# The end of a linear-attention and spectral-mixing kernel: eight tiles finished singly, the last mode's products with repeated columns, no 8 KB stores

## Chip, cores, metric

One core of one Trainium2 chip. The metric is the device time of one execution in microseconds (us), the median of several. A profile is one execution recorded instruction by instruction; its span (first to last instruction) is 1.7 to 1.8 us shorter than the device time. The granted clock is the share of its full clock that TensorE was given at a moment, as the profile records it (1.00 or 0.50 here). PE is TensorE, DVE is VectorE, ACT is ScalarE, POOL is GpSimd, SP issues the stores.

## The reference, cut to what matters

```python
# q, k, v: [8 batches, 8 heads, 576, 64];  w_r, w_i: [64 modes, 512, 512];  w_ch: [512, 512]
q_p, k_p = phi(q), phi(k)                       # elu + 1
num = q_p @ (k_p^T v);  den = q_p . sum(k_p) + 1e-6
x = (num / den)                                 # [8, 576, 512]
X = rfft(x, axis=1)[:, :64]                     # 64 modes
Y = X * (w_r + i w_i)                           # one 512x512 complex product for each mode
u = x + irfft(Y, n=576)
out = u + maximum(u @ w_ch, 0)                  # float32
```

The mode weights are 134 MB in float32. Loading them fills most of the time: their last packet lands at 387.69 us of 419.6. What is left after the last weights have landed is a chain: the last mode's product, its way through the inverse transform, the sums of all output tiles, and 9.4 MB of stores.

Of the kernel before, what the change touches and what calls it, by code (L numbers as in the profile page):

```python
# [10 lines left out]
F32 = mybir.dt.float32  # L11
# [32 lines left out]
def kernel(  # L44
# [10 lines left out]
    nc = tc.nc  # L55

    B, H, S, Dh = q.shape
    D = H * Dh
    NM = moe_w_r.shape[0]
    NHP = H // 2  # L60
    NDC = D // 128
    NJJ = 4
    NDW = 4 * NDC
    NDL = NDW // 2
    NMP = NM // 2
    XDC = 2 * B * NMP
    NL = 8
# [24 lines left out]
    def xt_cols(dc: int, kk: int, n: int):  # L92

        dc = (dc // NDC * 2 + kk % 2) * NDC + dc % NDC
        c0 = dc * XDC + kk // 2
        return xt_c[:, c0 : c0 + (n - 1) * NMP + 1 : NMP]
# [6 lines left out]

    W_KEEP = 2
    pin = tc.keep_in_program_order
    PIECES = (slice(0, 4), slice(4, 6), slice(6, 7), slice(7, 8))
    HALVES = [slice(0, 64), slice(64, 128)]

    LAST = NM // 2 - 1
# [11 lines left out]
    def w_load_last(pool, tag: str, bufs: int):  # L121
        w_in[LAST] = pool.tile([128, NDW, D], BF16, tag=tag, bufs=bufs, name=f"w{LAST}")
        for g in range(2):
            for half in range(2):
                rows_in = (moe_w_r, moe_w_i)[half][NM - 2 + g].rearrange("(p dc) e -> p dc e", dc=NDL)
                for dcs in PIECES if (g, half) == (1, 1) else (slice(0, NDL),):
                    dst = w_in[LAST][half::2, g * NDL + dcs.start : g * NDL + dcs.stop]
# [22 lines left out]
    def rows_of(jj: int, base: int = 0):  # L150

        if jj < NJJ:
            return slice(base + jj, base + 512, NJJ)
        return slice(512, S) if base == 0 else slice(0, base)
# [252 lines left out]
    def w_get(p: int):  # L407
        if p not in w_in and p == LAST:
            w_load_last(wpool, "w", W_KEEP)
        elif p not in w_in:  # L410
            for half in range(2):
                w_load(p, half, wpool, "w", W_KEEP)
        return w_in[p]

    def keep_warm(n: int):

        for _ in range(n):
            pin(nc.tensor.matmul(last_ps[0], id16, wch16[:, 0, :]))  # L418
# [4 lines left out]
    def work_slot(p: int, name: str):  # L423
        for _ in range(slots.get((p, name), 0)):
            if work:
                work.pop(0)()

    def product(P, x, n: int, w, dc: int, n_dc: int):
        c = dc % NDC * 32
        pin(  # L430
            nc.tensor.matmul(  # L431
                P[c : c + n, :], x, w[:, dc, :],
                start=(dc < NDC), stop=(dc >= n_dc - NDC), tile_position=(0, c),
                skip_group_check=True,
            )
        )
# [6 lines left out]
    def evacuate(p: int, P):  # L443
        st = ystage.tile([128, D], F16, tag="ystage", bufs=2, name=f"ys{p}")
        if p % 2 == 0:
            pin(nc.vector.tensor_copy(out=st, in_=P))  # L446
        else:
            pin(nc.scalar.copy(out=st, in_=P))  # L448
        return st

    def picks(kk: int, st, n: int):
        for ec in range(NDC):
            pin(
                nc.tensor.matmul(  # L454
                    yt_ps[:, ec, kk % 8 : kk % 8 + n, :].rearrange("p m n -> p (m n)"),
                    st[:, ec * 128 : ec * 128 + 128],
                    pick_sb[:, 0 : n * 2 * B],
                )
            )
# [24 lines left out]
    def last_pair():  # L484
        w = w_get(LAST)
        kk = NM - 2
        work_slot(LAST, "start")
        P = psW.tile([128, D], F32, tag="P", bufs=2, name=f"P{kk}")
        for dc in range(NDL):
            n = 32 if dc < NDC else 2 * B  # L490
            product(P, xt_cols(dc, kk, n), n, w, dc, NDL)
        st = evacuate(kk, P)
        work_slot(LAST, "mid")
        picks(kk, st, 1)
        pin(nc.vector.tensor_copy(out=Y8[:, :, 0 : NL - 1, :], in_=yt_ps[:, :, 0 : NL - 1, :]))
        keep_warm(3)
        kk = NM - 1
        y_last = psW.tile([128, NDC, 2 * B], F32, tag="P", bufs=2, name="y_last")
        for dc in range(NDL):
            for ec in range(NDC):  # L500
                pin(
                    nc.tensor.matmul(
                        y_last[:, ec, :], w[:, NDL + dc, ec * 128 : ec * 128 + 128],
                        xt_cols(dc, kk, 2 * B),
                        start=(dc == 0 and ec == 0), stop=(dc == NDL - 1), skip_group_check=True,
                    )
                )
        nc.vector.tensor_copy(out=Y8[:, :, NL - 1, :], in_=y_last)

    while pending:  # L510
        w_next()
# [7 lines left out]
    psW = tc.alloc_tile_pool(name="psW", bufs=1, space=PSUM, side="left")  # L519
# [13 lines left out]
    Y8 = ystage.tile([128, NDC, NL, 2 * B], F16, name="Y8")  # L533
# [27 lines left out]
    def x_of(t: int):  # L561
        if t < B * NJJ:
            return x_main[t // NJJ][:, t % NJJ, :]
        i = t - B * NJJ
        return x_tail[i // 2][:, i % 2, :]
# [37 lines left out]
    def parts_of(t: int):  # L603
        if t < B * NJJ:
            b, jj = divmod(t, NJJ)
            return [(b, jj, slice(0, 128))]
        p = t - B * NJJ
        return [(2 * p + h, NJJ, HALVES[h]) for h in range(2)]
# [123 lines left out]
    def add_inverse(n: int, half: int, tiles_of=(0, 1)):  # L732

        def mm(i, orow, l, r):
            on_bank(
                n, {i},
                nc.tensor.matmul(  # L737
                    accs[n][orow, i], l, r, start=False, stop=True, skip_group_check=True
                ),
            )  # L740

        for i in tiles_of:
            for b, jj, orow in parts_of(pairs[n][i]):
                sel_rows = rows_of(jj, BASE[b % 2])
                if n < 2 * N_LEAD:
                    mm(i, orow, lead_sb[b][:, sel_rows], last[:, half, :])
                else:
                    g = HALVES[i]
                    mm(i, orow, inv2_sb[g, sel_rows], YZ[b][g, half, :])

    pairs = []
# [9 lines left out]
    def on_bank(n: int, banks: set, ins):  # L761
        pin(ins)
        for other, theirs in users.setdefault(n, []):
            if not banks & theirs:
                tc.declare_no_dep(ins.ins, other.ins, reason="the other bank of the pair")
        users[n].append((ins, banks))
    accs: dict[int, object] = {}

    def channels(n: int):
        pool = acc_pools[n % 4 // 2]  # L770
        accs[n] = pool.tile([128, 2, D], F32, tag="acc", bufs=2, name=f"acc{n}")
        for i, t in enumerate(pairs[n]):
            for cols, src in e0_parts(t):
                on_bank(
                    n, {i},
                    nc.tensor.matmul(  # L776
                        accs[n][:, i, cols], id16, src, start=(cols.start == 0), stop=False,
                        skip_group_check=True,
                    ),
                )  # L780

    def rectified(n: int):
        add_inverse(n, 1)
        for i in range(2):
            a = accs[n][:, i]
            on_bank(n, {i}, nc.scalar.activation(out=a, in_=a, func=AF.Relu))
# [13 lines left out]
            in_=x_tail[i // 2],  # L800
        )

    QUADS = (6, 7)

    def finish(n: int):
        acc = accs[n]
        t0 = pairs[n][0]
        add_inverse(n, 0)
        x = x_main[t0 // NJJ][:, t0 % NJJ : t0 % NJJ + 2, :] if t0 < B * NJJ else x_tail[(t0 - B * NJJ) // 2]
        on_bank(n, {0, 1}, nc.vector.tensor_tensor(out=x, in0=acc, in1=x, op=ALU.add))  # L810
        if t0 < B * NJJ and t0 // NJJ in QUADS:
            if t0 % NJJ:
                store(t0 - 2, NJJ)
            return
        store(t0, 2)
# [106 lines left out]
    for h, eng in enumerate((nc.sync, nc.gpsimd)):  # L922
        eng.dma_start(
            out=YZ_all[64 * h : 64 * h + 64 : NF // NL].rearrange("r b z d -> r b (z d)"),
            in_=last.rearrange("p z d -> p (z d)"),
# [6 lines left out]
    def relu(n: int, i: int):  # L932
        a = accs[n][:, i]
        on_bank(n, {i}, nc.scalar.activation(out=a, in_=a, func=AF.Relu))

    def add_one(n: int, i: int):
        t = pairs[n][i]
        on_bank(n, {i}, nc.vector.tensor_tensor(out=x_of(t), in0=accs[n][:, i], in1=x_of(t), op=ALU.add))
        store(t, 1)

    add_inverse(0, 1, (1, 0))
    on_bank(
        0, {0},
        nc.vector.scalar_tensor_tensor(
            out=x_of(0), in0=accs[0][:, 0], scalar=0.0, in1=x_of(0), op0=ALU.max, op1=ALU.add
# [1 line left out]
    )  # L947
    store(0, 1)
    relu(0, 1)
    rectified(1)  # L950
    add_inverse(0, 0, (1,))
    channels(2)
    add_one(0, 1)
    rectified(2)
    for i in range(2):
        add_inverse(1, 0, (i,))
        add_one(1, i)
    channels(3)
    rectified(3)
    finish(2)  # L960
    for n in range(4, len(pairs)):
        channels(n)
        rectified(n)
        finish(n - 1)
# [32 lines left out]
```

## The kernel before: the parts that the change and the argument touch

The transformed x lies in one tile, with the modes innermost, so the 16 columns that belong to one mode (8 batches, real and imaginary) are 32 elements of two bytes apart:

```python
xt_c = xpool.tile([128, NDW * XDC], BF16, name="xt_c")
xt_v = xt_c.rearrange("p (c t b m) -> p c t b m", c=NDW, t=2, b=B)     # m innermost, NMP = 32 of them

def xt_cols(dc, kk, n):
    dc = (dc // NDC * 2 + kk % 2) * NDC + dc % NDC
    c0 = dc * XDC + kk // 2
    return xt_c[:, c0 : c0 + (n - 1) * NMP + 1 : NMP]                 # step NMP
```

The weights of the last mode come in pieces, and its products use the weights as the stationary operand and 16 columns as the moving one. Before the products stand three fillers (`keep_warm`: products of 128x512 whose result nobody reads):

```python
PIECES = (slice(0, 4), slice(4, 6), slice(6, 7), slice(7, 8))          # of 8 row blocks
...
        keep_warm(3)
        kk = NM - 1
        y_last = psW.tile([128, NDC, 2 * B], F32, tag="P", bufs=2, name="y_last")
        for dc in range(NDL):                                          # 8 row blocks
            for ec in range(NDC):                                      # 4 column blocks
                pin(nc.tensor.matmul(
                        y_last[:, ec, :], w[:, NDL + dc, ec * 128 : ec * 128 + 128],
                        xt_cols(dc, kk, 2 * B),
                        start=(dc == 0 and ec == 0), stop=(dc == NDL - 1), skip_group_check=True))
        nc.vector.tensor_copy(out=Y8[:, :, NL - 1, :], in_=y_last)
```

Then the tiles of the output are finished: tiles 0 to 3 one by one, all later ones in pairs (n numbers the pairs). `channels(n)` puts the product with w_ch into PSUM, `add_inverse(n, 1)` adds the last modes' share to it, `relu` rectifies, `add_inverse(n, 0)` adds the inverse transform, and `add_one` or `finish` adds all that to x and stores it. Pairs 0 and 1 (tiles 0 to 3) take the last mode from `last`, with 128 rows; later ones take it from `YZ`, with 64 rows: one product of a pair reads rows 0 to 63, the other rows 64 to 127, and in the trace the two start 4 ns apart (394.706 and 394.710 us, L737).

```python
    QUADS = (6, 7)                     # batches whose four tiles are stored in one 1 MB transfer
    ...
    store(0, 1)
    relu(0, 1)
    rectified(1)                       # add_inverse(1, 1) and relu for both tiles of the pair
    add_inverse(0, 0, (1,))
    channels(2)
    add_one(0, 1)
    rectified(2)
    for i in range(2):
        add_inverse(1, 0, (i,))
        add_one(1, i)
    channels(3)
    rectified(3)
    finish(2)
    for n in range(4, len(pairs)):
        channels(n)
        rectified(n)
        finish(n - 1)
    finish(len(pairs) - 1)
```

## Time and profile before

| | before |
|---|---|
| device time, first three runs | 421.33, 421.40, 422.91 us |
| span of the profiled execution | 419.6 us |
| last packet of the weights | 387.69 us |
| copy of the last mode's product starts | 388.32 us |
| first store of output issued | 391.68 us |
| VectorE's last sum ends | 413.73 us |
| last store packet ends | 418.22 us |

The rows are moments of one execution, counted from its first instruction. Read them as a chain: what the loads leave, the single file through the engines (388 to 391.7), and the stores. The prediction below shows the lines that these moments come from. Two lines more are needed for later, from the order of TensorE's instructions: four small products (`yt`, 16 columns of two bytes that lie side by side) and the 32 products of the last mode, 16 columns each. In the single instructions the first follow each other at 25 ns and the second at 28.

```profile
385.97 0.26 PE L454 MATMUL yt<-pick_sb,ys 128*128 128x16 f16 x4
386.79 1.50 PE L502 MATMUL y_last<-xt_c,w 128*128 128x16 bf16 x32
```

### The profile page before, as it was taken

What the parts mean: (1) busy time and instruction counts of PE and PEld (TensorE: products, weight loads), DVE (VectorE), ACT (ScalarE), POOL (GpSimd) and SP (SyncE); (2) the same over time, 40 slices, a digit from 0 to 9 for tenths busy, and PEclk for the clock granted to TensorE, in tenths of its full rate; (3) what the DMA queues carried; (4) which work ended last, traced back from release to release, by engine and by line L of the source; (5) the groups of instructions that cost most, each with busy time, mean ns of one, the idle gap of its engine ahead of it and who ended that gap; (6) DMA issues with size and microseconds to landing.
All of it is one profiled execution on the core that took longest, in us unless ns stands there. A gap on an engine that the chain in (4) does not pass through costs nothing.

```text
span 419.6 us, 7393 instructions
## 1 busy us (share of the span) xinstructions
PE 289.5 (69%) x3118; PEld 157.0 (37%) x3118; DVE 227.9 (54%) x495; ACT 154.1 (37%) x253; POOL 57.5 (14%) x99
## 2 busy tenths in 40 slices
PE   0359799999607553444343686998798877899992
PEld 0248677787301221222121232433343324364420
DVE  3588979994404462464645353454455433612794
ACT  4677788954101011000000233344253422230782
POOL 4122224210001111111111111111111111130000
PEclk9999958989555555555555589799899989999997
DMA  8999999999999999999999999999999999998698
GB/s 217 211 212 217 209 223 204 227 206 225 216 221 212 215 220 211 219 217 211 223 214 212 223 214 211 223 215 212 221 214 214 219 214 217 219 208 162 229 402 322
DMA packets 16417, 93.17 MB, mean 222 GB/s; under 512 B 2032, under 2 KB 2944, under 8 KB 11968
## 3 DMA queue, kind: packets, MB, share of 16 engines
q0 software_dynamic: 12416, 81.48, 93.3%
q1 hardware_dynamic: 3968, 11.22, 7.1%
q8 instruction: 24, 0.39, 0.3%
q14 instruction: 9, 0.07, 0.0%
HBM read 163.93 MB, written 9.44 MB: 413 GB/s over the span
## 4 chain that ended last, share of the span: by engine, by line
DMA 68%; PE 19%; DVE 4%; issue 3%; POOL 3%; ACT 2%; DVEq 0%; ACTq 0%; POOLq 0%
DMA w<-in_moe_w_i_dram 53%; DMA pick_sb<-row_pick 8%; PE P L431 7%; DMA k<-in_k_dram 7%; PE acc L737 3%; PE acc L776 2%; POOL w L116 2%; PE kvp L256 1%; ACT ke L207 1%; DVE x L292 1%; PE zl L418 1%; PE yt L454 1%; PE xp L322 0%; ACT ys L448 0%; PE num L162 0%
## 5 line engine op out<-in xcount | busy, mean ns | idle before, releaser
L431 PE MATMUL P<-w,xz 128*32 128x512 bf16 x496 | 48.3, 529 | 63.9 <-DMA w<-in_moe_w_i_dram 61.5
L448 ACT CAST ys<-P 128x512 f16<-128x512 f32 x15 | 8.8, 586 | 131.4 <-PE P L431 131.4
L116 POOL DMA_DIRECT2D w<-in_moe_w_r_dram x31 | 17.8, 576 | 244.1 <-PE P L431 240.6
L431 PEld LDWEIGHTS <-xz 128*32 128x32 bf16 x496 | 13.2, 115 | 85.0 <-DMA w<-in_moe_w_i_dram 56.4
L446 DVE CAST ys<-P 128x512 f16<-128x512 f32 x17 | 11.8, 691 | 54.1 <-PE P L431 54.1
L678 PE MATMUL eps<-wch,xTw 128*128 128x512 f16 x144 | 40.6, 409 | 0.0
L162 PEld LDWEIGHTS <-qT 64*128 64x128 f16 (+1 forms) x640 | 22.8, 124 | 31.7 <-issue 17.3
L661 ACT CAST x16w<-x_main 128x512 f16<-128x512 f32 x32 | 19.8, 618 | 37.6 <-DVE x_main L659 37.6
L659 DVE TENSOR_TENSOR x_main<-ya,x_main 128x512 f32<-128x512 f32 x32 | 22.0, 691 | 18.8 <-PE ya L655 18.6
L256 PE MATMUL kvp<-vpad,ke 32*128 32x130 f16 x576 | 23.4, 256 | 8.9 <-ACT qT L243 6.1
L441 DVE COPY xz<-xt_c 64x256 bf16<-64x256 bf16 x62 | 23.0, 370 | 11.5 <-PE P L431 10.7
L686 ACT CAST E<-eps 128x512 f16<-128x512 f32 (+1 forms) x40 | 21.2, 540 | 19.5 <-PE eps L678 19.5
L256 PEld LDWEIGHTS <-ke 32*128 32x128 f16 x576 | 21.5, 113 | 10.6 <-issue 8.5
L162 PE MATMUL nw<-kv,qT 64*128 64x65 f16 (+1 forms) x320 | 18.9, 240 | 9.5 <-DVE x_tail L622 4.5
L418 PE MATMUL zl<-wch,id 128*128 128x512 f16 x96 | 23.1, 380 | 0.0
L292 DVE TENSOR_TENSOR x<-num,rd 128x512 f16<-128x512 f32 x32 | 22.1, 692 | 1.1
L236 PE MATMUL qTp<-id,qe 128*128 128x128 f16 x144 | 14.2, 277 | 12.0 <-DVE qe L220 9.7
L207 ACT ACTIVATE qe<-q 128x1152 f16<-128x1152 f16 (+1 forms) x16 | 17.9, 1157 | 7.6 <-DMA q<-in_q_dram 7.5
L622 DVE TENSOR_TENSOR x_main<-nw,rd 128x256 f32<-128x256 f32 x32 | 11.2, 415 | 17.4 <-PE nw L162 17.4
L670 DVE COPY xTw<-xTp 128x512 f16<-128x512 f16 x36 | 15.0, 416 | 10.0 <-PE xTp L668 9.9
L454 PE MATMUL yt<-pick_sb,ys 128*128 128x32 f16 (+1 forms) x128 | 8.8, 186 | 16.2 <-DMA pick_sb<-row_pick 10.1
L243 ACT COPY qT<-qTp 128x1152 f16<-128x1152 f16 x16 | 19.6, 1289 | 0.4 <-PE qTp L236 0.2
(117 smaller groups left out, 492.9 us busy)
## 6 DMA issues: line engine op xcount, KB each, us to landing
w<-in_moe_w_r_dram POOLq DMA_DIRECT2D x31, 1024.0 KB, 12.5
w<-in_moe_w_i_dram POOLq DMA_DIRECT2D x31, 1024.0 KB, 16.8
out_dram<-x_main SPq DMA_DIRECT2D x10, 512.0 KB, 4.0
k<-in_k_dram POOLq DMA_DIRECT2D x8, 576.0 KB, 12.8
v<-in_v_dram POOLq DMA_DIRECT2D x8, 576.0 KB, 14.2
q<-in_q_dram POOLq DMA_DIRECT2D x7, 576.0 KB, 12.5
out_dram<-x_main SPq DMA_DIRECT2D x2, 1024.0 KB, 4.6
q<-in_q_dram SPq DMA_DIRECT2D x2, 576.0 KB, 4.7
```

Of the source, the lines that this page charges most:

```text
L116: nc.gpsimd.dma_start(out=w_in[p][half::2], in_=two.rearrange("g (r dc) e -> (g r) dc e", dc=NDW))
L162: mm = nc.tensor.matmul(num[hpo][orow, c0 : c0 + 65], qT[rows, hpp, h2, cols], kv_sb[rows, hpp, h2, :])
L207: pin(nc.scalar.activation(out=ev[:, c], in_=heads(nm, b, c), func=AF.Exp))
L256: nc.tensor.matmul(kv_ps[:, h2, 0:130], phi["k", b][r0 : r0 + 32, j // NJ, j % NJ].rearrange("p o d -> p (o d)"), vp[r0 : r0 + 32, :, j, 0 ...
L292: nc.vector.tensor_tensor(out=dst.rearrange("p (o c d) -> p o c d", o=2, c=4), in0=nv[:, :, :, 0:64], in1=rden.unsqueeze(3).broadcast_to([ ...
L418: pin(nc.tensor.matmul(last_ps[0], id16, wch16[:, 0, :]))
L431: nc.tensor.matmul(P[c : c + n, :], x, w[:, dc, :], start=(dc < NDC), stop=(dc >= n_dc - NDC), tile_position=(0, c), skip_group_check=True,)
L441: pin(nc.vector.tensor_copy(out=xz[p % 2][HALVES[h], :, h, :], in_=src))
L659: pin(nc.vector.tensor_tensor(out=x, in0=acc, in1=x, op=ALU.add))
L661: pin(nc.scalar.copy(out=x16w[t], in_=x))
L678: nc.tensor.matmul(e_ps, xT[:, c, :], wch16[:, c, :], start=(c == 0), stop=(c == NDC - 1))
L686: pin(nc.scalar.copy(out=dst, in_=e_ps[:, cols]))
```

## The change

Its parts: (1) tiles 0 to 7 are finished singly, with the sums made ahead by a few tiles, and pairs come after; (2) the last mode's products take their 16 columns six times over (96 columns, of which only the first 16 results are used), and a filler is put behind them; (3) the last piece list starts with two smaller pieces; (4) no batch waits for all four of its tiles to be stored in runs of 8 KB. What each part aims at is not written in the kernel; the names suggest that the repeats and the filler are to keep TensorE's clock up, and the singles to bring the stores forward.

```diff
-    PIECES = (slice(0, 4), slice(4, 6), slice(6, 7), slice(7, 8))
+    PIECES = (slice(0, 2), slice(2, 4), slice(4, 6), slice(6, 7), slice(7, 8))
@@
-        y_last = psW.tile([128, NDC, 2 * B], F32, tag="P", bufs=2, name="y_last")
+        n_rep = 6
+        y_last = psW.tile([128, NDC, n_rep, 2 * B], F32, tag="P", bufs=2, name="y_last")
         for dc in range(NDL):
+            x = xt_cols(dc, kk, 2 * B).unsqueeze(1).broadcast_to([128, n_rep, 2 * B])
             for ec in range(NDC):
                 pin(
                     nc.tensor.matmul(
-                        y_last[:, ec, :], w[:, NDL + dc, ec * 128 : ec * 128 + 128],
-                        xt_cols(dc, kk, 2 * B),
+                        y_last[:, ec], w[:, NDL + dc, ec * 128 : ec * 128 + 128], x,
@@
-        nc.vector.tensor_copy(out=Y8[:, :, NL - 1, :], in_=y_last)
+        keep_warm(1)
+        nc.vector.tensor_copy(out=Y8[:, :, NL - 1, :], in_=y_last[:, :, 0, :])
@@
-    QUADS = (6, 7)
+    QUADS = ()
@@  (channels() may now be called for one tile of a pair)
+    def sums_of(n: int, i: int):
+        channels(n, (i,))
+        add_inverse(n, 1, (i,))
+        relu(n, i)
@@
-    rectified(1)
-    add_inverse(0, 0, (1,))
-    ... (down to finish(2), as above)
+    for i in range(2):
+        add_inverse(1, 1, (i,))
+        relu(1, i)
+    singles = [(0, 1)] + [(n, i) for n in (1, 2, 3) for i in range(2)]
+    ahead = [(n, i) for n in (2, 3, 4) for i in range(2)] + [(5, 0)]
+    for n, i in singles:
+        add_inverse(n, 0, (i,))
+        if ahead:
+            sums_of(*ahead.pop(0))
+        add_one(n, i)
+    finish(4)
+    sums_of(5, 1)
+    for n in range(6, len(pairs)):
```

More of the change, by code (lines that the diff above doesn't have):

```diff
@@ L767, with channels @@
     accs: dict[int, object] = {}
-    def channels(n: int):
-        pool = acc_pools[n % 4 // 2]
-        accs[n] = pool.tile([128, 2, D], F32, tag="acc", bufs=2, name=f"acc{n}")
-        for i, t in enumerate(pairs[n]):
+    def channels(n: int, tiles_of=(0, 1)):
+        if n not in accs:
+            accs[n] = acc_pools[n % 4 // 2].tile([128, 2, D], F32, tag="acc", bufs=2, name=f"acc{n}")
+        for i in tiles_of:
+            t = pairs[n][i]
             for cols, src in e0_parts(t):
@@ L949 @@
     relu(0, 1)
-    rectified(1)
-    add_inverse(0, 0, (1,))
-    channels(2)
-    add_one(0, 1)
-    rectified(2)
-    for i in range(2):
-        add_inverse(1, 0, (i,))
-        add_one(1, i)
-    channels(3)
-    rectified(3)
-    finish(2)
-    for n in range(4, len(pairs)):
+    for i in range(2):
+        add_inverse(1, 1, (i,))
[10 more added lines that the diff above has]
+    for n in range(6, len(pairs)):
         channels(n)
```

## The prediction

> **What bounds the kernel now.** I read the page's slices first (where is the transfer side not full?), then the chain of waits, then stretches of the end, then the order of VectorE's work there.
>
> ```profile
> DMA  8999999999999999999999999999999999998698
> GB/s 217 211 212 217 209 223 204 227 206 225 216 221 212 215 220 211 219 217 211 223 214 212 223 214 211 223 215 212 221 214 214 219 214 217 219 208 162 229 402 322
> DMA 68%; PE 19%; DVE 4%; issue 3%; POOL 3%; ACT 2%; DVEq 0%; ACTq 0%; POOLq 0%
> ```
>
> For 37 of 40 slices (10.5 us each) the transfers are full. These are loads: 164 MB are read from memory at 413 GB/s over the span, and landed narrower. The dips are in slices 37, 38 and 40. The change edits nothing before the last pair of modes, so some 385 of the 421.4 us are out of its reach. In 1 us stretches the loads fall off from 384 on and end at 387.7; the stores run until 418.2. So I cut the end there:
>
> ```profile
> core 0: us, PE busy (x) PEld busy (x) DVE busy (x) ACT busy (x) POOL busy (x), PEclk, DMA share, GB/s
> 384.00:388.00 4.00, 3.96 (x50) 1.74 (x48) 1.32 (x2) 0.00 (x0) 0.00 (x0) 1.00 0.50 92
> 388.00:391.60 3.60, 3.02 (x23) 1.87 (x24) 1.85 (x4) 1.97 (x5) 0.57 (x1) 1.00 0.01 2
> 391.60:396.00 4.40, 4.40 (x21) 1.84 (x19) 3.55 (x6) 3.70 (x8) 0.00 (x0) 1.00 1.02 328
> 396.00:396.50 0.50, 0.50 (x5) 0.15 (x4) 0.50 (x1) 0.24 (x2) 0.00 (x0) 1.00 0.85 303
> 396.50:410.75 14.25, 14.25 (x82) 3.73 (x80) 14.14 (x13) 12.77 (x24) 0.00 (x0) 1.00 1.01 401
> 410.75:414.00 3.25, 1.26 (x8) 0.33 (x6) 2.94 (x3) 1.13 (x3) 0.00 (x0) 1.00 0.96 386
> 414.00:417.50 3.50, 0.00 (x0) 0.00 (x0) 0.00 (x0) 0.00 (x0) 0.00 (x0) 0.60 1.00 404
> ```
>
> The last two columns are to be read. From 388 to 391.6 nothing moves: the last mode's result goes through PE, DVE and ACT one after the other. From 391.6 to the end the transfers are full (1.02, 1.01, 1.00), short only at 396.0 (0.85) and around 411 to 414 (0.96). VectorE is also busy for 14.14 of 14.25 us. Which of the two sets the end? VectorE's last sum ends at 413.7, the transfers go on for 4 us more without a gap, so they do. The sums come in this order (start, duration):
>
> ```profile
> 391.79 0.69 DVE L938 TENSOR_TENSOR x_main<-acc,x_main 128x512 f32<-128x512 f32 x1
> 392.87 1.29 DVE L938 TENSOR_TENSOR x_main<-acc,x_main 128x512 f32<-128x512 f32 x2 [0.39 <-PE acc L737]
> 394.38 6.10 DVE L810 TENSOR_TENSOR x_main<-acc,x_main 128x1024 f32<-128x1024 f32 x5 [0.22 <-PE acc L737]
> ```
>
> One tile costs 0.69, a pair 1.22. A pair is 512 KB, so VectorE offers 524/1.22 = 430 GB/s and the stores take about 401: once behind, the stores stay behind. The hole at 396.0 is where they had caught up: the first whole pair was stored only at 395.63.
>
> And the last mode, in the chain of waits:
>
> ```profile
> 386.89 1.07 PE y_last L502 x28
> 388.00 0.30 PE y_last L502 x4
> 388.32 0.23 DVE Y L508
> ```
>
> In the single instructions, products start 28 ns apart, with breaks at 387.21 to 387.37, 387.59 to 387.67 and 387.77 to 387.99, each before the products of the next piece. The last piece's last packet ended at 387.69. So the last landing (387.99), not PE, sets this step.
>
> [...] the granted clock is 1.00 or 0.50, and it was 1.00 from 343 to 414.7. So in this execution a filler has nothing to win. [...] The trace has 28 ns at 16 columns and 56 ns at 128 [...] here 0.30 us lie between the last packet and its first product (387.69 to 387.99). [...] 84 ns for 2 KB, 160 for 4 KB, 312 for 8 KB (medians of the packet records).
>
> **The change part by part.**
>
> Smaller first pieces. The last 512 KB of weights come in 256, 128, 64, 64 KB; now the first is cut in two. In the packet records of that load, 4 KB packets took 324 ns and 2 KB packets 173, so each pair costs 22 ns more: 64 packets over 16 engines, 4 each, 0.09 us, and one more 22 ns semaphore write: +0.11 us on the last landing. What it gives: products of the first two of eight row blocks can start earlier. But PE works on the filler of three until 386.72, and the whole 256 KB piece had landed by 386.7, so nothing is gained there.
>
> Repeated columns. Six copies of the 16 columns: products 42.5 apart instead of 28.4. The 28 before the last landing still fit between landings (eight take 0.34 us; their room is 0.3). After the last landing: 3 x 14 ns, and 80 columns more to stream in the last product, 33 ns: +0.08 us. The filler, one product of 128x512 (0.22 us), lies in the 0.3 us in which PE waits for VectorE's copy: 0. Sum for the last mode: about +0.17 us (0.11 + 0.08, a little of it overlapped).
>
> Eight tiles singly. Today the singles are tiles 0 to 3, then 7 pairs and more. After: 7 additions of 0.69 (4.83) and 14 pairs of 1.22 (17.1), 21.9 us; before: 3 of 0.69 and 16 pairs, 21.6. So VectorE has 0.3 us more work, but loses its waits of 0.39 and 0.22, because the next tile's sums are now made between one tile's end and the next. PE needs about 3 x 0.215 = 0.65 us for a tile, just under 0.69. Net: VectorE ends within 0.3 us of where it did. For the stores: 256 KB come each 0.69 us, 380 GB/s, and behind the 512 KB rearrangement copies this is enough to keep a queue. The hole at 396 (0.85 of 0.5 us in the window; 12.3 and 9.2 of 16 engines in its two halves, so 0.16 us) and a shortfall at 397.75 (0.03) should go. The price: 4 tiles x 128 packets of 2 KB at 84 instead of half as many at 160: 512 x 4.3 ns / 16 = +0.14 us.
>
> No 8 KB runs. The hold-back of 1 MB ends, so the dips at 410.75 and 413.5 (0.08 + 0.03 us) should go. Price: 256 packets of 8 KB (mean 318) become 512 of 4 KB (164): 512 x 164 - 256 x 318, over 16: +0.16 us by means, +0.1 by medians.
>
> Sum: +0.17 (start of the stores) - 0.30 (holes) + 0.25 (packets) = +0.1 us.
>
> **Rivals.**
> First, that the transfers aren't the limit, but VectorE's stream with its two waits, or the wait for whole pairs. For it: VectorE is as full as the stores, and the chain of waits runs over PE and DVE from 390 to 413. Against it: 4 us of full transfers after its last sum. If true, the end moves by the waits and by the smaller last store (512 KB for 1 MB, 1.3 us): 420 to 420.5.
>
> Second, that timed runs often lose the clock here. For it: one of three runs took 422.91, 1.5 us more; half clock over the PE work from 388 to 394 would cost about that[...]. Against it: nobody profiled that run, and the median was a good one. If true, the median hardly moves and the high runs go: 421.0 to 421.4. The reverse is possible too: a median of three that draws two high ones reads 422.8.
>
> Third, that one late transfer engine sets the end. The stores' last semaphores come at 417.4 to 417.6 from most engines, but at 418.22 from one. The lag appears near 407 and 414, beside 8 KB instruction fetches. A busy engine can't make up for it, so filling holes helps this engine less, and its end would be 0.2 to 0.5 later: 421.7 to 421.9.
>
> **Range and chances.** The sum says 421.5. I lean 0.3 below, to 421.2, because the first two rivals both point down and such parts are seldom kept in a tuned kernel unless they paid. Each term is 0.1 to 0.3 us, the late engine adds 0.4 either way, and a clock lost in two runs adds 1.5: 420.2 to 422.2. A change of 2% is 8.4 us, while the whole edited stretch with empty or dipping transfers is under 6 us: faster by over 2% 0.01, slower 0.01, within 0.98.
>
> **What would show it.** Right: the last mode's copy to Y ends 0.1 to 0.2 later against the last landing; the transfers' share between 392 and 417 has no dip; single sums follow each other without waits; VectorE still ends 3 us or more before the stores. Wrong: the stores begin earlier than 3.9 us after the loads' last packet; VectorE's last sum is over 0.5 us earlier and the end follows it; the granted clock falls to 0.50 before the last stores; or the loads themselves end over 0.5 us elsewhere than at 387.7, which none of my steps foresees.

## The result, and the profile after

The changed kernel took 426.81 us (median of 6 runs, 426.27 to 430.75), the kernel before 421.41 us (6 runs, 421.33 to 423.26). The ratio is 1.0138, with a 95% interval of 1.0093 to 1.0184. Ratios here are the mean time of one kernel's fast runs over that of the other's of the same rounds, so not quite the ratio of the medians quoted. By the 2% rule that is "same", but 5.4 us slower is far outside the range on record.

| moment, us | before | after | difference |
|---|---|---|---|
| last packet of the weights | 387.69 | 387.64 | -0.05 |
| copy of the last mode's product starts | 388.32 | 392.02 | +3.70 |
| first store of output issued | 391.68 | 396.85 | +5.17 |
| VectorE's last sum ends | 413.73 | 420.08 | +6.35 |
| last store packet ends | 418.22 | 423.87 | +5.65 |
| span | 419.6 | 425.3 | +5.7 |

So the loads are unchanged and nothing is lost before them. Of 5.65 us, 3.70 are lost between the landing of the weights and the copy, another 1.47 on the way from the copy to the first store, and 0.48 among the stores. The chain of waits of the changed kernel names the first (start, us, what):

```profile
386.76 5.22 PE y_last L504 x32
391.98 0.43 PE zl L418
392.41 0.50 PE ypl L911 x4
392.91 0.85 PE zl L917 x4
393.76 0.85 PE z1l L917 x4
```

The 32 products took 5.22 us in one unbroken piece, where the prediction allowed them 42.5 ns each, 1.4 us. In the single instructions they start 163 or 164 ns apart (the first gap alone is 145), without a break for any piece of weights. The transposes behind them (`ypl`) took 0.50 and the two groups of four products 0.85 each, for 0.40, 0.44 and 0.45 before. The clock differs; two stretches of the changed kernel, the products and the way to the first store (the third column from the right is the granted clock):

```profile
core 0: us, PE busy (x) PEld busy (x) DVE busy (x) ACT busy (x) POOL busy (x), PEclk, DMA share, GB/s
386.60:391.80 5.20, 5.20 (x33) 3.71 (x32) 0.16 (x1) 0.00 (x0) 0.00 (x0) 0.86 0.08 13
391.98:396.35 4.37, 4.34 (x19) 2.22 (x18) 1.43 (x4) 1.70 (x4) 0.57 (x1) 0.50 0.00 0
```

PE reads as fully busy in both, and yet the clock was cut to 0.50 at 390.34, still within the slow products, and given back at 397.16. A busy share of 5.20 of 5.20 us did not keep the clock here. Note also that the products' spacing did not change at 390.34: at half the clock they were still 163 ns apart, while the products of 256 dense columns behind them (`zl`) started 213 ns apart at 0.50, for 109 at 1.00 in the kernel before. So the granted clock was not what paced the slow products.

In VectorE's order in the changed kernel (some lines between are left out), the first line is the copy, the rest are the tiles' sums:

```profile
392.02 0.22 DVE L510 CAST Y<-y_last 128x64 f16<-128x64 f32 x1 [5.26 <-PE y_last L504]
396.13 0.69 DVE L952 SCALAR_TENSOR_TENSOR x_main<-acc,x_main 128x512 f32<-128x512 f32 x1 [0.35 <-PE acc L739]
397.37 3.28 DVE L941 TENSOR_TENSOR x_main<-acc,x_main 128x512 f32<-128x512 f32 x5 [0.55 <-PE acc L739]
400.85 0.69 DVE L941 TENSOR_TENSOR x_main<-acc,x_main 128x512 f32<-128x512 f32 x1 [0.20 <-PE acc L739]
401.75 0.69 DVE L941 TENSOR_TENSOR x_main<-acc,x_main 128x512 f32<-128x512 f32 x1 [0.20 <-PE acc L739]
404.29 2.51 DVE L813 TENSOR_TENSOR x_main<-acc,x_main 128x1024 f32<-128x1024 f32 x2 [0.52 <-PE acc L739]
```

The bracket is VectorE's idle time before the line and what ended it. Five single sums do run back to back (3.28 us for five), as the change wants, but waits of 0.20, 0.20 and 0.52 us come after them, all for TensorE. This raises a second suspicion: is the new order of the end a cost of its own?

### The profile page after: what moved, and what is told of

Its sections match the earlier page's. It is cut to its first block, busy times and chain, and to the rows that moved or that the text cites.

```text
span 425.3 us, 7406 instructions
## 1 busy us (share of the span) xinstructions
PE 302.1 (71%) x3119; PEld 164.7 (39%) x3119; DVE 228.7 (54%) x497; ACT 154.7 (36%) x253; POOL 58.5 (14%) x100
## 4 chain that ended last, share of the span: by engine, by line
DMA 66%; PE 22%; DVE 3%; issue 2%; POOL 2%; ACT 2%; DVEq 0%; ACTq 0%; POOLq 0%
DMA w<-in_moe_w_i_dram 51%; DMA pick_sb<-row_pick 8%; PE P L431 7%; DMA k<-in_k_dram 7%; PE acc L739 3%; PE kvp L256 2%; PE acc L779 2%; POOL w L116 2%; PE y_last L504 1%; ACT ke L207 1%; PE qTp L236 1%; PE zl L418 1%; DVE x L292 1%; PE xf L354 1%; PE yt L454 0%
## 5 line engine op out<-in xcount | busy, mean ns | idle before, releaser
L256 PE MATMUL kvp<-vpad,ke 32*128 32x130 f16 x576 | 25.3, 273 | 8.8 <-ACT qT L243 5.9
L256 PEld LDWEIGHTS <-ke 32*128 32x128 f16 x576 | 23.4, 122 | 10.5 <-issue 8.6
L236 PE MATMUL qTp<-id,qe 128*128 128x128 f16 x144 | 16.0, 300 | 11.5 <-DVE qe L220 9.6
L162 PE MATMUL num<-kv,qT 64*128 64x65 f16 (+1 forms) x320 | 16.4, 222 | 5.2 <-DVE x L292 3.0
```

Source lines behind the costliest of these rows:

```text
L162: mm = nc.tensor.matmul(num[hpo][orow, c0 : c0 + 65], qT[rows, hpp, h2, cols], kv_sb[rows, hpp, h2, :])
L236: nc.tensor.transpose(qT_ps[:, j], phi["q", b][:, c, j].rearrange("p o d -> p (o d)"), id16,)
L256: nc.tensor.matmul(kv_ps[:, h2, 0:130], phi["k", b][r0 : r0 + 32, j // NJ, j % NJ].rearrange("p o d -> p (o d)"), vp[r0 : r0 + 32, :, j, 0 ...
```

## The experiments

Theories. A: the repeated columns cost nearly all of it. A1: because the moving operand's columns lie 64 bytes apart, each takes four times as long as a dense one; A2: because of the number of columns or the zero step of the repeat (the same addresses are read again). B: the new order of the end costs a good part. C: the half clock is a consequence of the slow products and costs about 2 us on top. The last mode's part and the rest of the change are separated first.

### 16 columns again, all else as changed (rep1)

```diff
-        n_rep = 6
+        n_rep = 1
```

> The changed kernel with the columns of the last mode's products not repeated (16 columns again, as before), all else as changed. Theory A (the 32 products with repeated columns cost the time: they took 5.2 us for 1.4, 163 ns each where I had estimated 42.5, and the half clock that followed came of it): 421.0 to 421.9 us, products 28 ns apart, clock 1.00 until the stores. Theory B (the new order of the end, singles for pairs, costs a good part, since VectorE waited after 400.6): 423.5 us or more.

Measured: 421.71 us (6 runs, 421.63 to 423.79) against 421.6, ratio 0.9995 [0.9964, 1.0026]. The products were 28 ns apart again, the copy started at 388.33, the first output store was issued at 391.69 and the clock stayed at 1.00 to 417. Theory A holds: without the repeats the loss is gone, and what the other parts do together is below what these runs resolve.

The run also isolates the order of the end, with the clock full. VectorE's order in this run:

```profile
391.80 3.28 DVE L941 TENSOR_TENSOR x_main<-acc,x_main 128x512 f32<-128x512 f32 x5
395.28 0.69 DVE L941 TENSOR_TENSOR x_main<-acc,x_main 128x512 f32<-128x512 f32 x1 [0.20 <-PE acc L739]
396.17 0.69 DVE L941 TENSOR_TENSOR x_main<-acc,x_main 128x512 f32<-128x512 f32 x1 [0.20 <-PE acc L739]
398.72 2.51 DVE L813 TENSOR_TENSOR x_main<-acc,x_main 128x1024 f32<-128x1024 f32 x2 [0.52 <-PE acc L739]
```

The waits of 0.39 and 0.22 at the first tiles are gone as predicted, but the same three new waits as above stand at later tiles. TensorE's order shows the reason:

```profile
394.19 0.38 PE L779 MATMUL acc<-E,id 128*128 128x512 f16 x1
394.50 0.40 PE L739 MATMUL acc<-YZ_all,inv_sb 64*128 64x512 f16 x1
394.84 0.41 PE L739 MATMUL acc<-last,lead_sb 128*128 128x512 f16 x1
395.08 0.38 PE L779 MATMUL acc<-E,id 128*128 128x512 f16 x1
```

From one `acc<-E` to the next, one tile's three products, pass 0.89 us (394.19 to 395.08); VectorE needs 0.69 for a tile. The product of 64 rows is what stretches it: 0.31 from the product before it and 0.34 to the next, where full products follow each other at 0.216. The kernel before has a pair at this place, whose two 64-row products start 4 ns apart:

```profile
394.71 0.41 PE L737 MATMUL acc<-YZ_all,inv_sb 64*128 64x512 f16 x2
395.05 0.62 PE L737 MATMUL acc<-last,lead_sb 128*128 128x512 f16 x2
```

The pair has the same 0.31 before it (the last `acc<-E` starts at 394.40) and the same 0.34 behind it. So the added time lies at the changes between 128 and 64 rows; a pair meets them once for two tiles, singles once for each. VectorE's last sum ended at 414.51, 0.78 later than before. The stores hid nearly all of it: their last packet ended at 418.37 against 418.22.

### The repeats alone on the kernel before (only_reps)

The edit is part (2) of the change alone, the repeats and the filler.

> The kernel before with the repeated columns and the filler behind them, nothing else of the change. Theory A: 426 to 427.5 us, nearly the whole loss, products 163 ns apart. Theory B: under 424.5 us, the rest being due to the order of the end.

Measured: 427.11 us (6 runs, 426.05 to 429.46), ratio 1.0125 [1.0091, 1.0159]. The products were 162 to 165 ns apart after a first gap of 145, and the clock fell to 0.50 at 392.77, again within the slow products. (The profiled execution, 429.46 us, is of a slower group of times that is explained below; its products began at 389.25.) Part (2) alone gives the whole loss; the other direction of the same statement as the run before, and theory B falls as an explanation of it.

### The same 96 columns from a dense tile (dense6)

```diff
+    xd = ystage.tile([128, NDL, 2 * B], BF16, name="xd")
+    for dc in range(NDL):
+        pin(nc.vector.tensor_copy(out=xd[:, dc, :], in_=xt_cols(dc, NM - 1, 2 * B)))    # long before
@@
-            x = xt_cols(dc, kk, 2 * B).unsqueeze(1).broadcast_to([128, n_rep, 2 * B])
+            x = xd[:, dc, :].unsqueeze(1).broadcast_to([128, n_rep, 2 * B])
```

> The changed kernel, but the 16 columns of each row block are first gathered into a dense tile (eight small VectorE copies long before), and the products repeat those six times: the same 96 columns, the same zero step of the repeat. Theory A1 (it is the 64-byte step between columns [...]): products 42 to 44 ns apart, 421.0 to 422.0 us, clock 1.00 through. Theory A2 (it is the number of columns, or the repeat itself): products still near 163 ns, 426 to 427.5 us.

Measured: 423.93 us median, but in two groups: 421.75 and 421.86, and four runs from 423.68 to 424.49; ratio 1.0023 [0.9992, 1.0055]. The median missed the expectation; the products did not. They start 41 to 47 ns apart, and the whole group takes 1.54 us:

```profile
389.52 1.54 PE L504 MATMUL y_last<-xd,w 128*128 128x96 bf16 x32
```

Same number of columns, same zero step for the repeats, a quarter of the time: A2 falls, A1 stands. The clock did not fall in the products or behind them: in this execution it was 1.00 from 372.6 to 416.9. But the products began at 389.52 instead of 386.7, before the changed line had any part in it. That is the second group of times, which the kernel before has too; more on it below.

### One row block for each step between columns (steps)

Eight groups of four products, each with columns at another step. Wide steps come from gathered tiles like the one above, with gaps.

```diff
+    steps = [1, 2, 3, 4, 8, 16, 32, 32]                 # in elements of two bytes
+        xs.append(ystage.tile([128, 2 * B, steps[dc]], BF16, name=f"xs{dc}")[:, :, 0])
+        pin(nc.vector.tensor_copy(out=xs[dc], in_=xt_cols(dc, NM - 1, 2 * B)))
@@  (row block 6 reads its 16 columns once, the others six times; the last two read xt_c itself)
```

> One look, for durations: as the changed kernel, but each of the eight row blocks reads its columns at another step: 1, 2, 3, 4, 8, 16 elements of two bytes from gathered tiles, then the original step of 32 with 16 columns, then with 96. Theory A1[...]: steps 1 to 4 at 42 to 44 ns a product, steps 8, 16 and 32 at about 163, and 28 for 16 columns at step 32. A rate that rises with the step (bandwidth of the bytes skipped) would give 2 elements near 80, 4 near 163 and 32 far more. Theory A2: all with 96 columns near 163. Total between 421.5 and 424.5 us.

TensorE's order in this run, one line for each row block:

```profile
386.67 0.34 PE L503 MATMUL y_last<-xs,w 128*128 128x96 bf16 x4
386.84 0.34 PE L507 MATMUL y_last<-xs,w 128*128 128x96 bf16 x4
387.02 0.43 PE L511 MATMUL y_last<-xs,w 128*128 128x96 bf16 x4
387.28 0.51 PE L515 MATMUL y_last<-xs,w 128*128 128x96 bf16 x4
387.61 0.86 PE L519 MATMUL y_last<-xs,w 128*128 128x96 bf16 x4
388.30 0.88 PE L523 MATMUL y_last<-xs,w 128*128 128x96 bf16 x4
388.99 0.29 PE L527 MATMUL y_last<-xt_c,w 128*128 128x16 bf16 x4
389.12 0.81 PE L531 MATMUL y_last<-xt_c,w 128*128 128x96 bf16 x4
```

The busy time of a group also holds the last product's run-out (0.34 us for four products that start 43 ns apart), so the start-to-start times of the single instructions are the better measure. The last two of the three in each group are given, since the first can still carry over from the step before:

| step, elements (bytes) | columns | start to start, ns | ns for one column |
|---|---|---|---|
| 1 (2) | 96 | 42 to 47 | 0.45 |
| 2 (4) | 96 | 42 to 44 | 0.45 |
| 3 (6) | 96 | 66 to 68 | 0.70 |
| 4 (8) | 96 | 86 to 87 | 0.90 |
| 8 (16) | 96 | 172 to 173 | 1.80 |
| 16 (32) | 96 | 174 | 1.81 |
| 32 (64) | 16 | 28 to 29 | 1.78 |
| 32 (64) | 96 | 163 to 164 | 1.70 |

The cost of a column is the same at 2 and 4 bytes (0.45 ns), grows with its step up to 16 bytes (1.80) and does not grow beyond (1.81 at 32, 1.70 at 64). Up to 16 bytes the table reads as about 0.11 ns for each byte of the step, but no less than the 0.45 of dense columns; that is an estimate from the row of 16 bytes (1.80 / 16), which gives 0.68 at 6 bytes and 0.90 at 8, where 0.70 and 0.90 were measured. Why it is so, these runs do not show. The time for a column did not follow the granted clock: in the changed kernel, at 64 bytes, it stayed the same at half the clock (163 ns a product). My expectation had steps 3 and 4 at 42 to 44 ns a product and missed there (66 to 68 and 86 to 87); the rate that would rise with the bytes skipped missed too. A2 falls once more. The row with 16 columns is the kernel before: its 28 ns are 16 columns at 1.78. They are not the shortest spacing: in the same traces the dense `yt` products start 25 ns apart, with 16 columns and with 32. The 28 lie only 3 ns above that, which is why they could pass for it. Why 16 and 32 bytes (173) are a little dearer than 64 bytes (163), no run shows. The time, 423.21 us in one run, lies in the expected range.

### Full-rate fillers in place of the slow products (filled)

```diff
-        n_rep = 6
+        n_rep = 1
@@
-        keep_warm(1)
+        keep_warm(18)
```

> The changed kernel with 16 columns, and 18 dense fillers of 128x512 (about 3.9 us of full-rate streaming) behind the last products instead of one, so that TensorE is kept as long as the slow products kept it, but densely. Theory C (the half clock after the slow products came because the array had little work in them, and cost about 2 us on top of their 3.7): the clock stays 1.00 until the stores are nearly done, 425.0 to 425.6 us in fast runs. Rival (the clock falls with the delay itself, or the half clock cost nothing): clock 0.50 again around the stores' start, or 426.5 us and more at full clock.

Measured: 425.15 us (6 runs, 424.98 to 425.28, and one of 428.88), ratio 1.0089 [1.0059, 1.0119]. Two stretches of this run, the fillers and the way to the first store:

```profile
388.00:392.00 4.00, 3.95 (x24) 1.88 (x23) 0.22 (x1) 0.00 (x0) 0.00 (x0) 1.00 0.00 0
392.00:395.00 3.00, 2.73 (x20) 1.68 (x18) 1.53 (x3) 1.88 (x5) 0.56 (x1) 1.00 0.00 0
```

TensorE was held up nearly as long as in the changed kernel (VectorE's first copy behind the transposes starts at 392.52, there at 392.95, 0.43 apart), but by dense products, and the clock stayed at 1.00 in both stretches. The last store packet ended at 422.02 against 423.87, 1.85 earlier. So the half clock cost at least 1.85 - 0.43, about 1.4 us (part of the 0.43 is half clock too: from the last mode's copy to that copy 0.93 us pass in the changed kernel, 0.71 in rep1), and it did not come of the delay itself. These are one profile each, but the times agree: five of six runs of filled lie at 425.0 to 425.3, and none of the changed kernel lies below 426.27. Theory C holds for the cause; its 2 us were too much.

### The order of the end alone (order_only), the 8 KB stores alone (quads_only)

The first is the new order with the old products, pieces and stores; the second is `QUADS = ()` alone.

> The kernel before with the new order of the end alone (eight tiles singly), old products, pieces and 8 KB stores. Theory D (VectorE's waits only move from the first tiles to tiles 6 to 10, and the stores are limited by the transfers anyway): 421.2 to 421.9 us in the fast state, VectorE's last sum 0.5 to 0.9 us later than before. Rival (the order was the useful part, masked by the products): under 421.0 us.

> The kernel before without the 8 KB stores alone. By the packets' durations +0.1 us of transfer time against 0.1 us of dips taken away: 421.2 to 421.7 us in the fast state. Rival (held-back stores cost at the end): under 421.0.

Measured: order_only 422.83 us (421.84, 421.90, 422.02 and 423.63 to 424.45), ratio 1.0022 [0.9997, 1.0047]; quads_only 422.47 us (421.72 to 421.84, and 423.09 to 425.41), ratio 1.0028 [0.9996, 1.0061]. Both medians mix the two groups of times. In the lower group order_only lies near 421.9 and quads_only near 421.8, where the kernel before lies at 421.3: neither helps, both may cost some 0.4 to 0.5 us, and with three such runs each this is not settled. That leaves order_only at the upper edge of what was expected and quads_only just above it. The profiles don't show such a cost: from the last mode's copy to the last store packet 30.05 us pass in order_only and 29.78 in quads_only, against 29.90 in the kernel before; and rep1, with both parts in it, lies 0.2 above the kernel before in the lower groups. VectorE's last sum comes 26.19 us after the copy in order_only, 0.78 later than before, as expected. For both, the rival that the part was useful on its own falls.

### A better order of the end (ahead3)

The kernel before, four tiles singly as there, sums made one tile ahead, and pairs from the third pair on, so that the 64-row products still come two by two (4 ns apart in the kernel before).

```diff
-    rectified(1)
-    add_inverse(0, 0, (1,))
-    ... (down to finish(2))
+    add_inverse(1, 1, (i,)); relu(1, i)                  # for i = 0, 1
+    add_inverse(0, 0, (1,)); sums_of(2, 0); add_one(0, 1)
+    add_inverse(1, 0, (0,)); sums_of(2, 1); add_one(1, 0)
+    add_inverse(1, 0, (1,)); sums_of(3, 0); add_one(1, 1)
+    add_inverse(2, 0);       sums_of(3, 1); finish_add(2)
```

> A candidate against both: the kernel before, four tiles singly as there, but the next sums made one tile ahead as in the change, and pairs from the third pair on, so that two products of 64 rows still run side by side. If single 64-row products caused VectorE's new waits: no VectorE wait over 0.2 us between 391.8 and 398, last sum 0.3 to 0.5 us earlier than before, no hole in the transfers at 396, 420.9 to 421.4 us. If the transfers alone set the end: the same as before within 0.2 us.

Measured: 422.3 us, lower group 421.31, 421.33, 421.58; ratio 1.0002 [0.9978, 1.0026]. The lower group is where the kernel before is. In the profiled execution (of the upper group) a wait of 0.54 us came back between the first and the second pair, and VectorE's last sum ended 25.41 us after the last mode's copy, just as in the kernel before. So the candidate moved VectorE's waits, but did not make it end 0.3 to 0.5 us sooner as the expectation had it; what a VectorE that ends sooner would be worth, this run does not show. The candidate is no better than the kernel before.

### The second group of times, and fewer fillers (fill44, fill00, fill855)

Over all rounds the kernel before had 39 runs: 26 from 421.19 to 421.70 and 13 from 422.47 to 424.08. All count as fast runs. The profiles of quads_only (its run took 425.24 us) and of before (421.32) show where they differ. First before, then quads_only, in the same three stretches:

```profile
359.00:373.00 14.00, 13.03 (x118) 7.14 (x110) 6.09 (x11) 4.95 (x9) 3.95 (x8) 1.00 1.03 219
373.00:386.00 13.00, 12.49 (x109) 6.76 (x110) 3.01 (x6) 2.09 (x4) 0.92 (x2) 1.00 0.93 191
```

```profile
359.00:373.00 14.00, 13.48 (x60) 4.32 (x50) 5.22 (x9) 3.51 (x6) 1.09 (x2) 0.52 1.03 220
373.00:386.00 13.00, 13.00 (x140) 8.58 (x139) 3.01 (x7) 3.51 (x6) 3.81 (x7) 0.99 0.91 182
```

In the slow one the clock was 0.52 from 359 to 373. TensorE did 60 products there instead of 118, made up for it from 373 on without a gap (13.00 of 13.00), and still began the last mode's products at 390.87, four microseconds late. The profiled executions of order_only, ahead3 and dense6 show the same: clock lost between 359 and 373, last products at 389.5 to 390.9, times of 424.5 to 425.2 (and that of only_reps: lost from 365.5 to 372.3, last products at 389.25). Those of before, rep1, filled and the changed kernel kept it there and began at 386.6 to 386.8. That is an agreement of profiles, not an intervention, and no slow execution of the kernel before itself was profiled; the next three runs were an intervention. They change only how many fillers follow mode pairs 28, 29 and 30 in the kernel before (5, 8, 8):

```diff
-    FILL = {..., 27: 9, 28: 5, 29: 8, 30: 8}
+    FILL = {..., 27: 9, 28: 5, 29: 4, 30: 4}      # fill44;  fill00: 5, 0, 0;  fill855: 8, 5, 5
```

> A candidate against both: the kernel before with 4 fillers instead of 8 after mode pairs 29 and 30. Theory E (the slow kind of run comes of a half clock somewhere from 352 to 373, after which TensorE has no idle time left, also because of these fillers, and reaches the last products 2.7 to 4 us late; fewer fillers give it back 8 x 0.22 = 1.7 us at full clock): the median stays at 421.3 to 421.6 and the slow kind of run comes down from 423 to 425 to about 421.5 to 423.5. Rival (the fillers are what holds the clock at the end): half clock after 375 and a median over 422.

> As the run with 4 fillers, but none after mode pairs 29 and 30. Theory E: slow runs down by up to 3.4 us, to 421.3 to 422, all runs within 1 us. Rival: the clock falls in the last two waits (some runs or all at half clock from 380 on), median 422.5 or more.

> As the run with 4 fillers, but 3 moved forward: 8 after mode pair 28 instead of 5, and 5 after 29 and 30. If the half clock can be kept away by more work around 365, slow runs get rarer; theory E alone gives 3 fillers' net relief, slow runs down by about 0.6 us, median 421.3 to 421.7.

Measured: fill44 421.64 us (five runs 421.46 to 421.74, one 422.73), ratio 1.0003 [0.9983, 1.0023]; fill00 422.43 us (422.00 to 423.47), 1.0023 [1.0002, 1.0045]; fill855 422.34 us (421.19 to 423.60), 1.0014 [0.9991, 1.0037]. The kernel before was at 421.28 in these rounds, with three of eleven runs at 423.1 to 423.5. The theory's half is borne out by one profile: in that of fill00 the clock was lost from 359.5 to 373.1, and the last products began at 387.31 all the same, not 390.9. So is the rival's half: in the profile of fill44 the clock fell at 388.40, on the chain itself:

```profile
385.00:388.40 3.40, 2.37 (x40) 1.45 (x39) 0.84 (x2) 0.00 (x0) 0.00 (x0) 1.00 0.38 68
388.40:391.80 3.40, 3.30 (x15) 2.03 (x16) 0.86 (x3) 1.12 (x3) 0.31 (x1) 0.50 0.00 0
```

In the profile of fill855 the clock fell at 388.44, too, and in both the first output store was issued at 392.86, 1.2 us later than before. In fill00, where TensorE was catching up after the earlier loss, it stayed at 1.00 to 414.1 without any of these fillers. By these three profiles fewer fillers trade one loss for another. None of the three beats the kernel before; the medians of fill44 (just) and fill855 (clearly) missed what the theory expected, fill00's runs were not within 1 us, and fill855's slow runs did not get rarer. The times of one kernel fall in two groups from execution to execution (26 and 13 runs of the kernel before), but the moment at which the clock was lost is known from one profile of each kernel only; what decides it was not tested.

## Why the prediction was wrong, point by point

**The step that failed** is "Repeated columns. Six copies of the 16 columns: products 42.5 apart instead of 28.4." They were 163.5 apart. The term was put at +0.08 us and measured +3.70 at the start of the copy. The 42.5 was the author's estimate, and it holds in this case for dense columns: they took 41 to 47 ns in dense6, and the line through the gaps of dense products before (56 ns at 128 columns, 109 at 256) gives 43 at 96. It was applied to columns 64 bytes apart without looking at how they lie. The trace of before held the clue: 28 ns at 16 columns was taken for the least that a short product takes, near the 25 ns of `yt`. Had it been divided by the columns, 28.4 / 16 = 1.78 ns, it would have said 170 ns for 96 columns, 32 x 170 = 5.4 us in all. Two readings fit one number, and only one was considered; the `yt` products in the same trace, 25 ns apart with 16 as with 32 dense columns, would have told them apart. That "the 28 before the last landing still fit between landings" fell with it.

**The clock.** "So in this execution a filler has nothing to win" was right for the kernel before. What was not asked is whether the change could lose the clock. It did: the clock fell at 390.34 within products that took 163 ns where dense ones took 43, and stayed at 1.00 in filled, where dense products held TensorE nearly as long. What in the slow products lowered it, no run shows. The loss was at least 1.4 us by the run with dense fillers. By the moments of before and after it is 1.8 (1.47 from the copy to the first store, and 0.48 among the stores less the 0.15 of the new order). The list of what would make the prediction wrong did name it ("the granted clock falls to 0.50 before the last stores").

**Sum of the loss.** 3.70 for the products, 1.47 for the way at half clock, 0.48 for the stores behind: 5.65, of a span longer by 5.7.

**What bounds the kernel.** Right. The loads ended within 0.05 us of where they did, and the stores set the end: in rep1 VectorE finished 0.78 us later, the stores 0.15. (The 413 GB/s that it gives for the reads include the writes; 164 MB in 419.6 us are 391.)

**Smaller first pieces, +0.11.** Not there: the last packet ended at 387.64 (after) and 387.65 (rep1) against 387.69.

**The filler behind the products, 0.** Right: in rep1 the time from the copy to the next one behind the transposes is 0.71 us (388.33 to 389.04), as before.

**Eight tiles singly.** "VectorE ends within 0.3 us of where it did": 0.78 later in rep1. The term mis-sized is "about 3 x 0.215 = 0.65 us for a tile"; it was 0.89, since each tile then pays for the changes to 64 rows and back (0.31 and 0.34 for 0.216), which a pair shares. Its "hole at 396" is sized at 0.16 us, but the share that it shows, 0.85 of 0.5 us, leaves only 0.08. "The hole at 396 should go" was right in part: the share at 396.0 to 396.5 rose from 0.85 to 1.14, but that from 396.5 to 410.75 fell from 1.01 to 0.98. The holes moved.

**No 8 KB runs, about 0.** By the lower runs of quads_only perhaps +0.4, by its profile nothing; not settled. The dips went, as foreseen: in rep1 the share from 410.75 to 414 is 1.02, for 0.96 before.

**The rivals.** That a lost clock makes the high runs is supported; that it is lost from 388 to 394 in the kernel before is not: the profiles of its variants put it at 359 to 373, and at 388.4 only with fewer fillers at the end. That the high runs would go with the change is refuted, for it is the change that lost the clock (0.50 from 390.34 to 397.16), and its runs reach 430.75. The first rival fell with rep1, where VectorE ended 0.78 us later and the stores only 0.15. The third, the late transfer engine, no run tests.

**The size of the rest.** The sum without the repeats was about 0.0 (0.1 less 0.08). rep1 measured 0.9995 [0.9964, 1.0026] in ratio, and 421.7 against 421.4 in the lower groups (medians). By these groups the rest of the sum was within half a microsecond.

## What to carry to other kernels

Before you widen a moving operand, look at the distance between its columns, and take a rate for one column from the products already in the trace. From one size alone, the 28 ns of a 16-column product here could be read as the least that any product takes or as 16 slow columns of 1.78 ns; a second size (163 ns at 96), or a dense product of the same size (25 ns), told which. If an operand must be read many times over, gather it into a dense tile beforehand: in dense6 that took the products from 163 ns to 43. It made up for the repeats there; that it beats 16 columns read in place, no run shows. And do not count on a product as a filler because it reads as busy: here the slow products read as fully busy (5.20 of 5.20 us) and the clock was lost all the same (0.50 from 390.34), while in filled it stayed at 1.00 with dense ones.
